# A chain of attention segments: the last outputs' scaling spread over two engines, and two VectorE steps exchanged

## The chip, the cores and the metric

The kernel runs on one core of a Trainium2 chip. A core has several engines, each with its own queue of instructions, worked off in the order in which the program issues them. TensorE (PE, with its weight loads as PEld) multiplies matrices and writes into PSUM, a memory of banks. VectorE (DVE), ScalarE (ACT) and GpSimd (POOL) work on elements; SyncE (SP) only issues transfers. An instruction that needs another engine's result waits on a semaphore, and everything behind it in its queue waits with it. The metric is the time of one execution on the device in microseconds (us), as the median of several.

## The reference

The program is four layers over a sequence of 2048 rows of 640 values: A, B, A, B, each with a layer norm before and a residual sum after. Layer A is attention with a recurrent memory; layer B is a linear attention. The change is in layer A, of which this is the core:

```python
for s in range(n_seg):                       # 64 segments of 32 rows
    h = jnp.concatenate([mem, xs], axis=1)   # 8 memory rows + 32 rows
    q, k, v = (einsum('btd,dhe->bhte', h, W) for W in (Wq, Wk, Wv))   # 32 heads of 192
    p = softmax(where(mask, einsum('bhqe,bhke->bhqk', q, k) * scale, -1e9))
    o = einsum('bhqk,bhke->bhqe', p, v)
    o = einsum('bhte,hed->btd', o, Wo)
    mem = o[:, :M, :]                        # the first 8 rows are the next segment's memory
    outs.append(o[:, M:, :])
```

The memory rows of one segment are an input of the next, so the 64 segments of a layer follow each other strictly, and there are two such layers: 128 segments in all.

## The kernel before, in words

The function `A_chain` (from L1052) runs the segments of a layer. Its instructions stand in each engine's queue in exactly the order of the program text (a manual schedule); waits are made by the framework from what each instruction reads and writes.

A segment handles its 32 heads in four rounds of eight (`NR = 4`, `L = NR - 1` is the last). All rounds share a few buffers. `hT` holds the segment's memory rows and part of its own rows, transposed. In a round, `project` (L1154) multiplies `hT` with the weights for queries, keys and values into the banks `ps_qk_q`, `ps_qk_k` and `ps_v`. `to_rows` (L1172) copies queries and keys out on ScalarE into `raws`, and `turn_rows` (L1177) transposes them in 32x32 blocks on VectorE into `QK` (whose halves are `KT` and `QT`). `scores` (L1194) multiplies them, `weigh` (L1276) takes the exponential into `E` on ScalarE.

The values of a round are cast out of their bank by `v_rows`: half of the bank's partitions (64 rows) by ScalarE (L1184), the other half by VectorE (L1186), both into the tile `Vp`. `attend` (L1207) multiplies `E` with `Vp`; a further column of ones gives the sum of the weights. In the first three rounds the two halves G = 0 and 1 of the outputs lie in one bank `ps_o`; in the last round each has a bank of its own (`ps_o`, and `ps_o1` in the place of the value bank). `weigh_rows` takes the reciprocals of the sums (L1227, in the last round L1231, first G = 1, then G = 0). `scaled` multiplies the outputs with them on their way into `raws`; it has a branch for ScalarE (L1237) and one for VectorE (L1239), which no call used so far. `turn` then transposes the outputs on VectorE (L1372 for the first and third round in one instruction, L1380 for the second and last in two, 192 columns each), and `wo_round` (L1266) multiplies them with the output weights, summed over all rounds into the bank `ps_w`. For the last round's outputs this is 24 products (`ps_w<-arena,QK`): first the 12 that read half G = 1, then the 12 of G = 0. Each half has three chunks of 64 columns; the first four products read the first chunk of G = 1.

The end of a segment is, in the order of the text: the third round's outputs are scaled on ScalarE, turned (L1423, in VectorE's queue as L1372) and the last values are cast (L1424); the last scores and exponentials; 24 products with the second round's outputs and others; `hx_transpose` (L1104), which turns the next segment's own rows into the next `hT`; the last `attend`; the reciprocals; the two scalings (L1440); `keep_values` (L1307), a ScalarE copy that SP then stores; the last turn; 24 products with the third round's outputs (`ps_w<-arena,raws`); the 24 products with the last; in 110 of 128 segments a product for later rows (`next_values`, `ps_x`). Then VectorE turns the memory rows out of `ps_w` (L1453) and adds their two halves into the next `hT` (L1455), and the next segment's queries begin.

The weights that don't stay on the chip are streamed by SP's queue all through the chain, each load released at a set step of TensorE; GpSimd's queue issues the small transfers (`kqb`, `Vp` tails, `xr`, `otb`).

Of the kernel before, what the change touches and what calls it, by code (L numbers as in the profile page):

```python
# [122 lines left out]
class Kernel:  # L123
# [928 lines left out]
    def A_chain(self, xn_dram, at_dram, li, load_slot, piece, late_wo, load_both, wo, low):  # L1052
        nc, tc, KC, NSEG = self.nc, self.tc, self.KC, self.NSEG
        scale = float(self.Dh) ** -0.5
        NR = 4
        with tc.tile_pool(name=f"A{li}_ch", reuse_waits="tile", bufs=1) as sp, \
# [40 lines left out]
            def rounds(s):  # L1097
                return range(NR) if s % 2 == 0 else range(NR - 1, -1, -1)
# [33 lines left out]
            def extra_v(s, n):  # L1132
                r = rounds(s)[n]
                nc.gpsimd.dma_start(out=Vs[n % 2][64:80, :],  # L1134
                                    in_=self.vb_d[s // 8, r].rearrange("g (t s) x f -> s (g t) (x f)", s=8)[s % 8])
# [43 lines left out]
            def v_rows(pv, n, engines):  # L1179
                for x in range(2):  # L1180
                    o = self.two_heads(Vs[n % 2][0:64, 2 * VH * x:2 * VH * x + 2 * VH])
                    i = self.spaced(pv[64 * x:64 * x + 64, 0:384])
                    if engines[x] == "s":
                        nc.scalar.activation(out=o, in_=i, func=ACT.Copy)  # L1184
                    else:
                        nc.vector.tensor_copy(out=o, in_=i)  # L1186
# [47 lines left out]
            def scaled(out, O, rc, G, eng):  # L1234
                i = O[G][:, VH * G:VH * G + 192]
                if eng == "s":
                    nc.scalar.activation(out=out, in_=i, func=ACT.Copy, scale=rc[G])  # L1237
                else:
                    nc.vector.tensor_scalar(out=out, in0=i, scalar1=rc[G], scalar2=None, op0=ALU.mult)  # L1239
# [9 lines left out]
            def tail_rows(rc, rows):  # L1249
                nc.scalar.activation(out=rows, in_=pair[0][:, 0:192], func=ACT.Copy, scale=rc)  # L1250
                return rows
# [80 lines left out]
            for s in range(NSEG):  # L1332
                W = pop.tile([P, 512], F32, name="ps_w", tag="w")
                order = rounds(s)
                L = NR - 1

                def q_or_k(m, n, halves=False):
                    ps = psk if m == "K" else psq
                    project(hT, ps, m, n, s, range(KC))
                    return to_rows(ps, m, halves)  # L1340

                def v_banks():
                    return pop.tile([P, 512], F32, name="ps_v", tag="v")

                def tails_after(n):
                    if n + 2 < NR:
                        extra_v(s, n + 2)
                    elif s + 1 < NSEG:
                        extra_v(s + 1, n + 2 - NR)

                if s > 0:
                    keep_rows(W_done)
                    rows = tail_rows(rct, spare_rows())
                    otb = turn_tail(rows)
                    store_rows(s - 1)
                    store_tail(otb, s - 1, rounds(s - 1)[L])
                turn_rows(q_or_k("Q", 0))
                turn_rows(q_or_k("K", 0))
                pv = v_banks()
                project(hT, pv, "V", 0, s, range(KC))  # L1360
                if s == 0:
                    late_wo(2)
                    late_wo(3, range(OWN // 2))
                v_rows(pv, 0, "sv")
                turn_tails(s)
                OTs = []

                def turn(n, osc):
                    if n in (0, 2):
                        rows = (raw_of["K"][:, 0:384] if n else ots).rearrange("p (c j) -> p c j", j=64)  # L1370
                        OTs.append([rows[:, 3 * G:3 * G + 3, :] for G in range(2)])
                        nc.vector.transpose(out=rows, in_=osc.rearrange("p (c j) -> p c j", j=64))  # L1372
                        return
                    if n == L:
                        OTs.append([KT[:, 3 * G:3 * G + 3, 0:64] for G in range(2)])
                    else:
                        OTs.append([vt[:, VH * G:VH * G + 192].rearrange("p (c j) -> p c j", j=64) for G in range(2)])
                    parts = osc if n == L else [osc[:, 192 * G:192 * G + 192] for G in range(2)]
                    for v, part in list(zip(OTs[n], parts))[::-1 if n == L else 1]:
                        nc.vector.transpose(out=v, in_=part.rearrange("p (c j) -> p c j", j=64))  # L1380

                outs = [(j, i) for j in range(L) for i in range(0, 12 if j else OWN, 2)]

                def output_steps(n):
                    for j, i in outs[0:n]:
                        wo_round(W, order[j], OTs[j], False, False, range(i, i + 2))
                    del outs[0:n]

                for n in range(L):
                    raw = q_or_k("Q", n + 1)  # L1390
                    if n == 2:
                        otb = turn_tail(otr)
                    E = weigh()
                    next_kq(s, n)
                    turn_rows(raw)
                    if n == 1:
                        step = wo_round(W, order[0], OTs[0], True, False, range(OWN, 12))
                        if s == NSEG - 1:
                            load_both(order[L], True)
                            self.kept_tails = []  # L1400
                            self.release(step, 12)
                            tails = self.kept_tails
                        else:
                            load_both(order[L], False)
                    raw = q_or_k("K", n + 1, n + 1 == L)
                    O = attend(E, n)
                    if n != 2:
                        tails_after(n)
                    fetch_kq(s, n)
                    if n == 2:  # L1410
                        store_tail(otb, s, order[1])
                    rc = weigh_rows(O)
                    if n == 1:
                        rct = weigh_tail()
                    turn_rows(raw)
                    if n == L - 1:
                        output_steps(STEPS[0])
                    pv = v_banks()
                    project(hT, pv, "V", n + 1, s, range(KC))
                    osc = raw_of["Q"][:, 0:384]  # L1420
                    for G in range(2):
                        scaled(osc[:, 192 * G:192 * G + 192], O, rc, G, "s")
                    turn(n, osc)  # L1423
                    v_rows(pv, n + 1, "sv")  # L1424
                    if n == 1:
                        otr = tail_rows(rct, raw_of["K"][:, 0:192])
                E = weigh(E)
                tails_after(2)
                next_kq(s, L)
                output_steps(STEPS[1])  # L1430
                if s + 1 < NSEG:
                    hT = new_hT()
                    hx_transpose(hT)
                O = attend(E, L)
                tails_after(L)
                fetch_kq(s, L)
                rc = weigh_rows(O)
                oscs = [raw_of["Q"][:, 192 * G:192 * G + 192] for G in range(2)]
                for G in (1, 0):
                    scaled(oscs[G], O, rc, G, "s")  # L1440
                keep_values()
                turn(L, oscs)
                output_steps(len(outs))
                if s == NSEG - 1:
                    self.spread_tails(0, tails[0], low, "vv")
                if s + 2 < NSEG:
                    load_rows(s + 2)
                wo_round(W, order[L], OTs[L], False, True, (*range(6, 12), *range(6)))
                load_tails(s + 1)
                next_values(s)  # L1450
                if s + 1 < NSEG:
                    wt = raws[:, 0:640].bitcast(F32).rearrange("p (a b t) -> p a b t", a=2, b=KC)
                    nc.vector.transpose(out=wt, in_=W[:, 0:320].rearrange("p (a j b) -> p a b j", a=2, b=KC))  # L1453
                    for a in range(2):
                        nc.vector.tensor_tensor(out=hT[64 * a:64 * a + 64, :, 0:8], in0=wt[0:64, a, :, 0:8],  # L1455
                                                in1=wt[64:P, a, :, 0:8], op=ALU.add)
                rct = weigh_tail()
                W_done = W
# [92 lines left out]
```

## Time and profile before

| what | value |
|---|---|
| median of 3 runs | 3152.37 us (3149.12 to 3162.98) |
| the profiled execution's own time | 3147.72 us |
| its span | 3146.0 us |
| mean granted TensorE clock | 0.993 |
| time from one segment's L1453 to the next, quickest ones | 17.94 us |

The profile is of one execution. A line of the page's groups gives the source line, engine and operation, the tiles written and read, the shapes and the count; behind the first bar the busy time in us and the mean duration of one in ns; behind the second the time that the engine had been idle just before, and who released it. A line of a timeline gives start and duration in us from the start of the span, an `xN` for merged neighbours, and in brackets the idle time before with its releaser. A line of the chain of waits gives start and duration of one piece of the path that ended last. A line of the waits gives who waited for whom, the total in us, how often, and the longest. Durations of products overlap, since TensorE starts the next before the last has come out.

### The profile page before, as it was taken

What the parts mean: (1) busy time and instruction counts of PE and PEld (TensorE: products, weight loads), DVE (VectorE), ACT (ScalarE), POOL (GpSimd) and SP (SyncE); (2) the same over time, 40 slices, a digit from 0 to 9 for tenths busy, and PEclk for the clock granted to TensorE, in tenths of its full rate; (3) what the DMA queues carried; (4) which work ended last, traced back from release to release, by engine and by line L of the source; (5) the groups of instructions that cost most, each with busy time, mean ns of one, the idle gap of its engine ahead of it and who ended that gap; (6) DMA issues with size and microseconds to landing.
All of it is one profiled execution on the core that took longest, in us unless ns stands there. A gap on an engine that the chain in (4) does not pass through costs nothing.

```text
span 3146.0 us, 141467 instructions
## 1 busy us (share of the span) xinstructions
PE 2989.4 (95%) x59552; PEld 1917.3 (61%) x59586; DVE 2180.7 (69%) x5420; ACT 1909.3 (61%) x4540; POOL 1388.6 (44%) x2867
## 2 busy tenths in 40 slices
PE   9899999999999999899999999999999999998999
PEld 7666666666666666555377666666666666665553
DVE  5577777777777777566644677777777777775665
ACT  3366666666666666556433666666666666665553
POOL 3255555555555555430112555555555555554300
PEclk9999999999999999999999999999999999999999
DMA  9877777877777787830378777777777777778300
GB/s 378 314 246 260 264 255 253 267 259 244 263 262 252 244 269 259 290 122 1 119 261 321 251 254 267 259 242 261 263 254 249 260 262 250 260 261 292 110 1 34
DMA packets 331783, 741.78 MB, mean 236 GB/s; under 512 B 67186, under 2 KB 108394, under 8 KB 328076
## 3 DMA queue, kind: packets, MB, share of 16 engines
q1 hardware_dynamic: 262252, 629.72, 57.8%
q0 software_dynamic: 68032, 99.38, 10.9%
q8 instruction: 469, 7.68, 1.0%
q10 hardware_dynamic: 864, 3.64, 0.3%
q14 instruction: 166, 1.36, 0.1%
HBM read 662.90 MB, written 70.14 MB: 233 GB/s over the span
## 4 chain that ended last, share of the span: by engine, by line
PE 76%; DVE 8%; DMA 8%; issue 3%; ACT 3%; POOL 1%; SPq 0%; DVEq 0%; POOLq 0%; ACTq 0%
PE ps_qk_k L1154 13%; PE ps_qk_q L1154 13%; PE ps_v L1154 12%; PE ps_w L1266 10%; PE ps_s L1194 6%; PE ps_pre L981 6%; PE ps_o L1207 2%; PE kv L1506 2%; DMA arena<-in_A_Wo_dram 2%; PE ps_wo L466 2%; DVE raws L1453 2%; ACT raws L1237 2%; DVE hT L1455 2%; PE ps_pq L517 2%; PE ps_t L1220 1%
## 5 line engine op out<-in xcount | busy, mean ns | idle before, releaser
L1154 PEld LDWEIGHTS <-hT 128*32 128x32 bf16 x30720 | 786.3, 96 | 458.3 <-DVE hT L1455 78.9
L1177 DVE STREAM_TRANSPOSE QK<-raws 128x512 bf16<-128x512 bf16 (+1 forms) x1152 | 729.6, 642 | 202.5 <-ACT raws L1172 164.1
L1130 POOL COPY QK<-kqb 64x192 bf16<-64x192 bf16 x1024 | 350.8, 343 | 468.7 <-PE ps_s L1194 261.5
L1154 PE MATMUL ps_qk_q<-arena,hT 128*32 128x384 bf16 x10240 | 509.9, 327 | 36.6 <-DVE hT L1455 28.2
L1154 PE MATMUL ps_qk_k<-arena,hT 128*32 128x384 bf16 x10240 | 509.7, 327 | 3.7 <-issue 2.8
L1172 ACT ACTIVATE raws<-ps_qk_k 128x512 bf16<-128x512 f32 (+1 forms) x640 | 313.6, 511 | 252.0 <-PE ps_qk_k L1154 245.1
L1237 ACT ACTIVATE raws<-ps_o,under 128x192 bf16<-128x192 f32 x1024 | 374.5, 421 | 113.3 <-DVE under L1231 98.5
L1154 PE MATMUL ps_v<-arena,hT 128*32 128x384 bf16 x8192 | 429.5, 326 | 6.2 <-issue 3.8
L1134 POOL DMA_DIRECT2D Vp<-vb x512 | 258.3, 504 | 326.3 <-PE ps_t L1220 214.8
L1172 ACT ACTIVATE raws<-ps_qk_q 128x512 bf16<-128x512 f32 x512 | 305.9, 598 | 156.7 <-PE ps_qk_q L1154 142.9
L1123 POOL DMA_DIRECT2D kqb<-kqb x512 | 292.8, 572 | 84.1 <-POOL QK L1130 59.4
L1186 DVE CAST Vp<-ps_v 64x384 bf16<-64x384 f32 x512 | 286.2, 559 | 25.3 <-ACT Vp L1184 9.2
L1194 PEld LDWEIGHTS <-QK 128*80 128x80 bf16 x4096 | 195.3, 120 | 167.6 <-issue 156.8
L1266 PE MATMUL ps_w<-arena,under 128*32 128x320 bf16 x6144 | 280.4, 300 | 4.9 <-issue 2.6
L1184 ACT ACTIVATE Vp<-ps_v 64x384 bf16<-64x384 f32 x512 | 247.0, 483 | 35.9 <-PE ps_v L1154 34.6
L1194 PE MATMUL ps_s<-QK 128*80 128x80 bf16 x4096 | 252.3, 209 | 5.3 <-DVE QK L1177 4.6
L1276 ACT ACTIVATE E<-ps_s 80x320 bf16<-80x320 f32 x512 | 217.9, 426 | 28.9 <-PE ps_t L1220 28.8
L1119 POOL DMA_DIRECT2D attn<-under x128 | 91.7, 716 | 265.9 <-DVE under L1115 231.2
L981 PEld LDWEIGHTS <-arena 128*128 128x128 bf16 x1920 | 187.9, 98 | 31.3 <-issue 4.1
L1112 ACT ACTIVATE raws<-ps_w 64x160 f32<-64x160 f32 x256 | 76.8, 300 | 205.9 <-DVE raws L1453 204.4
L1207 PE MATMUL ps_o<-Vp,E 80*32 80x193 bf16 x4096 | 179.6, 247 | 8.1 <-issue 3.9
L1266 PE MATMUL ps_w<-arena,QK 128*32 128x320 bf16 x3072 | 135.0, 304 | 36.2 <-DVE QK L1380 23.6
(166 smaller groups left out, 4362.1 us busy)
## 6 DMA issues: line engine op xcount, KB each, us to landing
arena<-in_A_Wo_dram SPq DMA_DIRECT2D x560, 320.0 KB
arena<-in_A_Wq_dram SPq DMA_DIRECT2D x427, 384.0 KB
arena<-in_A_Wk_dram SPq DMA_DIRECT2D x298, 384.0 KB
arena<-in_A_Wv_dram SPq DMA_DIRECT2D x290, 384.0 KB
kqb<-kqb POOLq DMA_DIRECT2D x512, 48.0 KB, 4.3
kqb<-arena POOLq DMA_DIRECT2D x14, 1536.0 KB, 9.5
Vp<-vb POOLq DMA_DIRECT2D x512, 24.2 KB, 3.6
otb<-otb POOLq DMA_DIRECT2D x256, 48.0 KB, 4.0
```

What stands on the lines that cost most here:

```text
L981: nc.tensor.matmul(ps[:, T * i:T * i + T], lhsT=w[b][:, P * c:P * c + P], rhs=xBT[:, b, :], start=(b == 0), stop=(b == KC - 1))
L1123: nc.gpsimd.dma_start(out=kqb[:], in_=self.kqb_d[r, :, s, :])
L1130: nc.gpsimd.tensor_copy(out=o, in_=kqb[h, :].rearrange("p (x c q) -> p x c q", c=3, q=16))
L1134: nc.gpsimd.dma_start(out=Vs[n % 2][64:80, :], in_=self.vb_d[s // 8, r].rearrange("g (t s) x f -> s (g t) (x f)", s=8)[s % 8])
L1154: last = nc.tensor.matmul(o, lhsT=hT[:, b, :], rhs=rhs, start=(i == 0), stop=(i == KC - 1), tile_position=(0, 32 * g), skip_group_check=True)
L1172: nc.scalar.activation(out=raw[:, c], in_=ps[:, c], func=ACT.Copy)
L1177: nc.vector.transpose(out=o, in_=i)
L1184: nc.scalar.activation(out=o, in_=i, func=ACT.Copy)
L1186: nc.vector.tensor_copy(out=o, in_=i)
L1194: nc.tensor.matmul(S[0:80, c0:c0 + 80], lhsT=KT[:, 4 * x + c, :], rhs=QT[:, 4 * x + c, :], start=(c % 2 == 0), stop=(c % 2 == 1), skip_gro ...
L1237: nc.scalar.activation(out=out, in_=i, func=ACT.Copy, scale=rc[G])
L1266: step = nc.tensor.matmul(W[q:q + 32, 0:320], lhsT=OT[i // 6][:, i % 6 // 2, 32 * (i % 2):32 * (i % 2) + 32], rhs=rhs, start=(first and i ...
```

## The change

Three edits, all in the end of a segment:

- In the round before the last, the cast of the last round's values (`v_rows`) is issued ahead of the turn of the third round's outputs instead of behind it. In VectorE's queue the two change places; on ScalarE nothing changes place, as the turn has no part there.
- Of the last outputs, half G = 1 is scaled by VectorE (a `tensor_scalar` out of PSUM with the reciprocal as a column), half G = 0 still by ScalarE.
- The turn of half G = 1 is made in two instructions, first the chunk of 64 columns that the first products read, then the other 128 columns; half G = 0 in one as before.

```diff
-                    for v, part in list(zip(OTs[n], parts))[::-1 if n == L else 1]:
-                        nc.vector.transpose(out=v, in_=part.rearrange("p (c j) -> p c j", j=64))
+                    pieces = ((1, 0, 1), (1, 1, 3), (0, 0, 3)) if n == L else ((0, 0, 3), (1, 0, 3))
+                    for G, a, b in pieces:
+                        nc.vector.transpose(out=OTs[n][G][:, a:b, :], in_=parts[G].rearrange("p (c j) -> p c j", j=64)[:, a:b, :])
...
                         scaled(osc[:, 192 * G:192 * G + 192], O, rc, G, "s")
+                    if n + 1 == L:
+                        v_rows(pv, n + 1, "sv")
                     turn(n, osc)
-                    v_rows(pv, n + 1, "sv")
+                    if n + 1 < L:
+                        v_rows(pv, n + 1, "sv")
...
                 for G in (1, 0):
-                    scaled(oscs[G], O, rc, G, "s")
+                    scaled(oscs[G], O, rc, G, "v" if G else "s")
```

## The prediction

> **What bounds the kernel now.** I read the page first, then the chain of waits of one segment, then the timelines of VectorE, ScalarE and TensorE over the end of that segment.
>
> ```profile
> span 3146.0 us, 141467 instructions
> PE 2989.4 (95%) x59552; PEld 1917.3 (61%) x59586; DVE 2180.7 (69%) x5420; ACT 1909.3 (61%) x4540; POOL 1388.6 (44%) x2867
> PE 76%; DVE 8%; DMA 8%; issue 3%; ACT 3%; POOL 1%; SPq 0%; DVEq 0%; POOLq 0%; ACTq 0%
> ...
> L1266 PE MATMUL ps_w<-arena,QK 128*32 128x320 bf16 x3072 | 135.0, 304 | 36.2 <-DVE QK L1380 23.6 <-DMA arena<-in_A_Wo_dram 8.8 <-issue 3.3
> ```
>
> TensorE is busy for 95% of the span and carries 76% of the chain. An edit on VectorE and ScalarE therefore matters only where TensorE stands still for them. The last row is such a place: the products with the last outputs of a segment (`ps_w<-arena,QK`, 24 in each of 128 segments). The chain through the end of one segment, start and duration in us:
>
> ```profile
> 615.58 0.18 PE ps_o L1207 x4
> 615.76 0.02 issue
> 615.78 0.26 DVE under L1231 x2
> 616.05 0.43 ACT raws L1237
> 616.48 0.02 issue
> 616.50 0.39 DVE QK L1380
> 616.89 0.04 issue
> 616.93 1.03 PE ps_w L1266 x24
> 617.96 0.02 issue
> 617.99 0.53 DVE raws L1453
> ```
>
> From the last attention product the path leaves TensorE for two reciprocals, one scaling on ScalarE and one turn (a 32x32 block transpose) on VectorE, comes back for the 24 products, and then goes to the turn that makes the next segment's memory rows. The same stretch on VectorE, on ScalarE and on TensorE:
>
> ```profile
> 613.35 0.77 DVE L1177 STREAM_TRANSPOSE QK<-raws 128x256 bf16<-128x256 bf16 x2
> 614.25 0.58 DVE L1372 STREAM_TRANSPOSE raws<-raws 128x384 bf16<-128x384 bf16 x1
> 614.86 0.56 DVE L1186 CAST Vp<-ps_v 64x384 bf16<-64x384 f32 x1
> 615.34 0.35 DVE L1104 STREAM_TRANSPOSE hT<-xr 128x160 bf16<-128x160 bf16 x1
> 615.78 0.25 DVE L1231 RECIPROCAL under<-ps_o 128x1 f32<-128x1 f32 x2
> 616.50 0.69 DVE L1380 STREAM_TRANSPOSE QK<-raws 128x192 bf16<-128x192 bf16 x2 [0.47 <-ACT raws L1237]
> 617.99 0.52 DVE L1453 STREAM_TRANSPOSE raws<-ps_w 128x320 f32<-128x320 f32 x1 [0.79 <-PE ps_w L1266]
> 618.54 0.43 DVE L1455 TENSOR_TENSOR hT<-raws 64x40 bf16<-64x40 f32 x2
> ```
> ```profile
> 613.48 0.74 ACT L1237 ACTIVATE raws<-ps_o,under 128x192 bf16<-128x192 f32 x2
> 614.19 0.48 ACT L1184 ACTIVATE Vp<-ps_v 64x384 bf16<-64x384 f32 x1
> ...
> 616.05 0.73 ACT L1237 ACTIVATE raws<-ps_o,under 128x192 bf16<-128x192 f32 x2 [0.74 <-DVE under L1231]
> 616.67 0.49 ACT L1307 ACTIVATE under<-ps_x 128x384 bf16<-128x384 f32 x1
> ```
> ```profile
> 615.47 0.35 PE L1207 MATMUL ps_o<-Vp,E 80*32 80x193 bf16 x8
> ...
> 615.72 1.00 PE L1266 MATMUL ps_w<-arena,raws 128*32 128x320 bf16 x24
> 616.93 1.00 PE L1266 MATMUL ps_w<-arena,QK 128*32 128x320 bf16 x24 [0.21 <-DVE QK L1380]
> ```
>
> Three things are to be seen. VectorE runs from 613.35 almost without a break to 615.69 (615.34 + 0.35) and is free only 0.09 before the reciprocals. From there on everything hangs on it and on ScalarE. And TensorE could start its last 24 products earlier than they come: 24 products take 1.00 with about 0.30 for the last alone, so six groups of four start 0.14 apart, and after 615.72 the next slot would be at 615.72 + 6 x 0.14 = 616.56. They start at 616.93, so 0.37 a segment is the most that a faster end can win.
>
> **The change part by part.** *Last values' cast ahead of the third outputs' turn.* On VectorE L1186 goes ahead of L1372. Nothing is added, no DMA moves, ScalarE's order stays. What counts is what the cast waits for. Its other half, L1184, reads the same bank `ps_v` on ScalarE. In the typical segment ScalarE's half ends at 614.67 and VectorE's starts at 614.86, with the turn in between as cover. A segment whose values came late shows it uncovered, and behind it stands the group of all these casts with its idle time and releaser:
>
> ```profile
> 1293.94 0.58 DVE L1372 STREAM_TRANSPOSE raws<-raws 128x384 bf16<-128x384 bf16 x1
> 1295.37 0.56 DVE L1186 CAST Vp<-ps_v 64x384 bf16<-64x384 f32 x1 [0.85 <-ACT Vp L1184]
> ```
> ```profile
> 1294.85 0.48 ACT L1184 ACTIVATE Vp<-ps_v 64x384 bf16<-64x384 f32 x1 [0.94 <-PE ps_v L1154]
> ```
> ```profile
> L1186 DVE CAST Vp<-ps_v 64x384 bf16<-64x384 f32 x512 | 286.2, 559 | 25.3 <-ACT Vp L1184 9.2
> ```
>
> The bank was full before 1294.85, since ScalarE read it then; VectorE was idle and still waited until ScalarE's half was done (1295.33) and 0.04 more. So the two halves go one after the other in this program, and the turn that now fills the wait is moved behind it. In the typical segment: VectorE is free at 614.12 and waits; the cast starts at 614.67 + 0.03 = 614.70, only 0.16 sooner. The next turn starts 0.48 behind a cast (614.86 to 615.34), at 615.18, and ends at 615.76; its reader, the products of 615.72, starts at 615.81, which costs nothing as TensorE has 0.37 to spare. Two turns of 0.378 together take 0.69, so one overlaps the next by 0.07: the turn of the next rows (L1104) starts at 615.18 + 0.58 - 0.07 = 615.69 and ends at 616.04. The reciprocals, behind it in VectorE's queue, start at 616.07 instead of 615.78: **0.29 later**. What they waited for before (TensorE's attention, 615.76) is no longer last. The attention itself, which waits for the cast's end (615.42 + 0.05 = 615.47), may start 0.05 sooner, which is then hidden.
>
> *Scaling side by side and the turn in two pieces.* Prices from these rows:
>
> ```profile
> L1380 DVE STREAM_TRANSPOSE QK<-raws 128x192 bf16<-128x192 bf16 x256 | 88.4, 378 | 59.3 <-ACT raws L1237 59.3
> L1372 DVE STREAM_TRANSPOSE raws<-raws 128x384 bf16<-128x384 bf16 x128 | 74.0, 578 | 17.1 <-ACT raws L1237 2.3
> L492 DVE TENSOR_TENSOR arena<-ps_v,rk 128x500 bf16<-128x500 f32 x64 | 40.8, 655 | 3.5 <-PE ps_v L466 3.3
> L492 DVE TENSOR_TENSOR arena<-ps_v,rk 128x140 bf16<-128x140 f32 x64 | 16.0, 292 | 0.0
> ```
>
> No VectorE scaling out of PSUM at 192 columns is in the trace. The nearest rows are products out of PSUM: 292 at 140 columns and 655 at 500, so 292 + 52 x 1.01 = 0.345; I take 0.35, with 0.29 and the 0.56 of the cast as outer bounds. Turns cost 1.04 ns a column (578 - 378 over 192), so 64 columns take 0.245 and 128 take 0.31; a piece could cost as little as 0.18 (0.245 less the overlap) and no more than the 0.378 of the undivided one. [...]
>
> New end, with 0.03 from one VectorE step to one that needs it (618.51 to 618.54): scaling 616.07 + 0.17 + 0.03 = 616.27 to 616.62; first piece 616.65 to 616.90; second 616.83 to 617.14; the other half's turn 617.07 to 617.45 (ScalarE's scaling, about 616.43 to 616.85, is done). TensorE, 0.05 behind each: first group 616.95, second and third 617.19 and 617.33, fourth 617.50, sixth 617.78. Before, the sixth started at 616.93 + 5 x 0.14 = 617.63. **0.15 later**. The second part alone would have won about 0.13 (the same sum from 615.78 gives 617.49); the first gives back 0.29. ScalarE's L1307, on whose end a store in SP's queue waits, moves from 616.67 to about 616.75, and SP's loads behind it by as much; POOL's load into `xr` comes over 1 us behind L1104 and is covered.
>
> ```profile
> PE ps_w L1266 <- DVE QK L1380: 23.6, 106, 0.8
> PE ps_w L1266 <- DMA arena<-in_A_Wo_dram: 12.8, 17, 2.8
> SPq L261 <- ACT under L1307: 460.6, 110, 5.5
> ```
>
> In 106 segments TensorE waited for the last turn; in others weights came last, and there a later turn costs nothing. 106 x 0.15 = 16 us. The profiled execution took 3147.7 us (span 3146.0); the sum is 3164. The median of the runs shown, 3152.4, lies 4.7 above it, so I give 3169.
>
> **The rivals.** *1. The cast does not really wait for ScalarE's half.* Then it runs beside it at 614.20, the turn ends at 615.26, L1104 at 615.54, the attention starts 0.05 earlier and so do the reciprocals, and the second part keeps its gain: 0.13 + 0.05 = 0.18 by 106, so 19 us less: 3133. Against it: the row with 0.85 of idle. For it: in the typical segment the cast's start is explained by the turn alone. It decides when the cast can start before about 614.40. [...]
>
> *2. The delay is absorbed.* A weight load late in one segment gets 0.15 more, so TensorE's other waits for DMA shrink; or the new VectorE steps are at their low ends (0.29 and 0.18), which takes 0.06 + 0.06 off. Then 0.03 a segment or nothing: 3152 to 3157, no measurable change. For it: DMA waits stand in the rows above; against it: they touch few segments.
>
> *3. The scalings are not side by side.* Both write `raws`, as the two casts both write `Vp`. If ScalarE's half waits for VectorE's, it runs from 616.68 to 617.10, the last turn starts at 617.13, and 0.06 more is lost: 106 x 0.21 = 22 us, 3175. With the scaling at 0.56 as well, 0.42 a segment: 3197.
>
> **How the numbers follow.** A change under 0.5% (16 us) can't be told from none here, and my likeliest value stands on that border. Chances: longer hand-over as summed, 0.08 to 0.25 a segment (3161 to 3179) 0.60, a little over half of it beyond the border; rival 3 or dearer VectorE steps (3175 to 3197) 0.16; absorbed 0.14; rival 1 0.10. So slower 0.33 + 0.16 and a little for a slow second part, 0.50; no change 0.27 + 0.14 - 0.01, 0.40; faster 0.10. The range goes from 3146, which leaves rival 1 out, to 3192, which leaves out the dearest steps. The likeliest case's own range is 3161 to 3179.
>
> **What would show it.** Right: the idle time before L1186 grows from 25 us to about 95 (0.70 - 0.12 = 0.58 in most of 128 segments), released by ScalarE's L1184; reciprocals L1231 start right behind L1104, with no idle time released by TensorE; a VectorE scaling of about 0.35; first piece about 0.245; TensorE's waits for the last turn grow. Wrong: the cast starting beside L1184, or reciprocals as early as before, or the last 24 products spread over less than 0.85.

## The result and the profile after

The changed kernel takes 3160.5 us (median of 22 runs) against 3155.4 us for the kernel before on the same chips; the ratio is 1.0024, 95% interval 1.0013 to 1.0036, so 4 to 11 us more, about 7.5 by the ratio (the two medians alone lie 5.1 apart). The change makes the kernel a little slower, by less than half a percent. The profiled execution has a span of 3152.3 us at a granted clock of 0.992.

The chain of waits through the end of one segment of the changed kernel (start, duration, engine and line):

```profile
617.00 0.47 ACT Vp L1184
617.46 0.02 issue
617.49 0.56 DVE Vp L1186
618.05 0.48 DVE raws L1372
618.53 0.24 DVE hT L1104
618.77 0.03 issue
618.80 0.23 DVE under L1231 x2
619.03 0.40 DVE raws L1239
619.43 0.02 issue
619.46 0.26 DVE QK L1381
619.71 0.04 issue
619.75 1.08 PE ps_w L1266 x24
```

Before, the last attention product on TensorE (`ps_o`) led straight to the reciprocals. Now the chain comes to them through ScalarE's half of the cast, VectorE's half, the third outputs' turn and the turn of the next rows, one behind the other in VectorE's queue. The timeline of VectorE over the same stretch shows what it waits for:

```profile
616.13 0.77 DVE L1177 STREAM_TRANSPOSE QK<-raws 128x256 bf16<-128x256 bf16 x2
617.49 0.56 DVE L1186 CAST Vp<-ps_v 64x384 bf16<-64x384 f32 x1 [0.58 <-ACT Vp L1184]
617.97 0.56 DVE L1372 STREAM_TRANSPOSE raws<-raws 128x384 bf16<-128x384 bf16 x1
618.46 0.31 DVE L1104 STREAM_TRANSPOSE hT<-xr 128x160 bf16<-128x160 bf16 x1
618.80 0.23 DVE L1231 RECIPROCAL under<-ps_o 128x1 f32<-128x1 f32 x2
619.00 0.42 DVE L1239 TENSOR_SCALAR raws<-ps_o,under 128x192 bf16<-128x192 f32 x1
619.46 0.70 DVE L1381 STREAM_TRANSPOSE QK<-raws 128x64 bf16<-128x64 bf16 x3
620.86 0.52 DVE L1457 STREAM_TRANSPOSE raws<-ps_w 128x320 f32<-128x320 f32 x1 [0.71 <-PE ps_w L1266]
```

VectorE now stands idle for 0.58 until ScalarE's half is done, and the work that used to fill this time follows later. The hand-over to the next segment (L1457, L1453 before) comes at 620.86; the one before it in this trace came at 602.83, 18.04 earlier. In the kernel before an undisturbed segment took 17.94 (600.05 to 617.99). The groups of the lines concerned:

```profile
L1186 DVE CAST Vp<-ps_v 64x384 bf16<-64x384 f32 x512 | 286.2, 559 | 100.6 <-ACT Vp L1184 88.8
L1266 PE MATMUL ps_w<-arena,QK 128*32 128x320 bf16 x3072 | 141.2, 305 | 29.7 <-DVE QK L1381 16.0 <-DMA arena<-in_A_Wo_dram 9.5 <-issue 3.1
L1239 DVE TENSOR_SCALAR raws<-ps_o,under 128x192 bf16<-128x192 f32 x128 | 53.5, 418 | 0.0
L1381 DVE STREAM_TRANSPOSE QK<-raws 128x192 bf16<-128x192 bf16 x128 | 42.9, 335 | 0.0
L1104 DVE STREAM_TRANSPOSE hT<-xr 128x160 bf16<-128x160 bf16 x126 | 39.0, 310 | 0.0
L1381 DVE STREAM_TRANSPOSE QK<-raws 128x128 bf16<-128x128 bf16 x128 | 34.4, 269 | 0.0
L1381 DVE STREAM_TRANSPOSE QK<-raws 128x64 bf16<-128x64 bf16 x128 | 31.4, 246 | 4.4
L1231 DVE RECIPROCAL under<-ps_o 128x1 f32<-128x1 f32 x256 | 30.3, 160 | 8.6 <-PE ps_o L1207 4.9
```

The idle time ahead of the casts went from 25.3 to 100.6 us, 88.8 of it released by ScalarE's half. That ahead of the reciprocals fell from 24.8 to 8.6, and the part of it that TensorE's attention released from 16.3 to 4.9: TensorE was waited for 42 times before and 11 times now, and in most segments they stand right behind L1104. The wait in the kernel before:

```profile
DVE under L1231 <- PE ps_o L1207: 16.3, 42, 1.6
```

In what follows, a *quick segment* is the shortest time that recurs from one hand-over to the next: the median of those within 0.05 us of the quickest, of the 124 intervals within the two layers. I take it as the time of a segment in which nothing is late. It repeats to 0.01 us (four of the kernels were run again with other loads, see below, and gave the same values), while the whole time of the kernel scatters by some 20 us between runs. Quick segments and their number come from one profiled execution of each kernel; the ratio is to the kernel before on the same chip, and where its interval holds 1 the whole time can't be told from that of the kernel before.

| kernel | quick segment | how many of 124 | ratio to before, 95% interval |
|---|---|---|---|
| before | 17.94 | 40 | 1 |
| changed | 18.04 | 46 | 1.0024 (1.0013 to 1.0036) |
| only the cast ahead of the turn | 18.175 | 37 | 1.0072 (1.0051 to 1.0092) |
| only the new end | 17.80 | 26 | 0.9975 (0.9962 to 0.9987) |
| only the scaling on two engines | 17.88 | 26 | 0.9998 (0.9984 to 1.0012) |
| only the turn in two pieces | 17.86 | 25 | 0.9975 (0.9959 to 0.9990) |
| changed, values in a second bank | 17.74 | 28 | 0.9959 (0.9943 to 0.9976) |
| second bank, old order, new end | 17.78 | 23 | 0.9974 (0.9956 to 0.9991) |
| changed, rows' turn late | 17.80 | 18 | 0.9991 (0.9977 to 1.0005) |

### The profile page after: what moved, and what is told of

The parts are those of the page before. It is cut to its first block, busy times and chain, and to the rows that moved or that the text cites. A ratio compares the mean times of both kernels' runs of the same rounds, so it can differ in the third digit from the quotient of the medians.

```text
span 3152.3 us, 141500 instructions
## 1 busy us (share of the span) xinstructions
PE 3009.4 (95%) x59586; PEld 1895.3 (60%) x59586; DVE 2210.4 (70%) x5676; ACT 1869.1 (59%) x4412; POOL 1391.7 (44%) x2867
## 4 chain that ended last, share of the span: by engine, by line
PE 71%; DVE 13%; DMA 7%; ACT 5%; issue 3%; POOL 1%; SPq 0%; DVEq 0%; POOLq 0%; ACTq 0%
PE ps_qk_k L1154 13%; PE ps_qk_q L1154 13%; PE ps_v L1154 10%; PE ps_w L1266 8%; PE ps_pre L981 5%; PE ps_s L1194 5%; DMA arena<-in_A_Wo_dram 2%; PE kv L1510 2%; DVE raws L1457 2%; PE ps_wo L466 2%; PE ps_o L1207 2%; ACT raws L1237 2%; DVE hT L1459 2%; DVE Vp L1186 2%; PE ps_pq L517 2%
## 5 line engine op out<-in xcount | busy, mean ns | idle before, releaser
L1237 ACT ACTIVATE raws<-ps_o,under 128x192 bf16<-128x192 f32 x896 | 334.5, 422 | 149.8 <-DVE under L1231 133.5
L1186 DVE CAST Vp<-ps_v 64x384 bf16<-64x384 f32 x512 | 286.2, 559 | 100.6 <-ACT Vp L1184 88.8
L1184 ACT ACTIVATE Vp<-ps_v 64x384 bf16<-64x384 f32 x512 | 247.0, 482 | 34.4 <-PE ps_v L1154 33.3
## 6 DMA issues: line engine op xcount, KB each, us to landing
Vp<-vb POOLq DMA_DIRECT2D x512, 24.2 KB, 3.7
```

## The experiments

My theory was that the change is two effects of opposite sign: the exchange of cast and turn makes what stands behind them in VectorE's queue late, since the cast waits for ScalarE's half; the new end wins back about half. The first rival was that the exchange is harmless and the new end costs the time.

**The two parts alone.** The exchange alone:

```diff
+                    if n + 1 == L:
+                        v_rows(pv, n + 1, "sv")
                     turn(n, osc)
-                    v_rows(pv, n + 1, "sv")
+                    if n + 1 < L:
+                        v_rows(pv, n + 1, "sv")
```

> The kernel before with the last values' cast ahead of the third outputs' turn and nothing else. In the traces, quick segments take 17.94 us in the kernel before and 18.04 in the changed one. Theory (the cast waits for ScalarE's half, so what is queued behind it on VectorE comes late): the last reciprocals start 0.24 later as in the changed kernel, and with the old end all of it reaches the hand-over: quick segments 18.15 to 18.20, the time 15 to 30 us above before. Rival (the exchange is harmless, the new end with its VectorE scaling and three turns costs the time): quick segments 17.94, no change within 5 us.

Measured: quick segments 18.175 and 1.0072, 23 us. The timeline of VectorE in this kernel has the old end behind the late reciprocals:

```profile
606.82 0.56 DVE L1186 CAST Vp<-ps_v 64x384 bf16<-64x384 f32 x1 [0.58 <-ACT Vp L1184]
607.30 0.56 DVE L1372 STREAM_TRANSPOSE raws<-raws 128x384 bf16<-128x384 bf16 x1
607.79 0.31 DVE L1104 STREAM_TRANSPOSE hT<-xr 128x160 bf16<-128x160 bf16 x1
608.13 0.23 DVE L1231 RECIPROCAL under<-ps_o 128x1 f32<-128x1 f32 x2
608.85 0.69 DVE L1380 STREAM_TRANSPOSE QK<-raws 128x192 bf16<-128x192 bf16 x2 [0.48 <-ACT raws L1237]
610.34 0.52 DVE L1456 STREAM_TRANSPOSE raws<-ps_w 128x320 f32<-128x320 f32 x1 [0.80 <-PE ps_w L1266]
```

The reciprocals come 15.98 behind the last hand-over (592.15 to 608.13) instead of 15.73 (600.05 to 615.78), and all of these 0.24 to 0.25 reach the next hand-over (610.34 - 592.15 = 18.19, against 17.94; 0.235 over the quick segments). The rival falls. The other part alone:

```diff
-                    for v, part in list(zip(OTs[n], parts))[::-1 if n == L else 1]:
-                        nc.vector.transpose(out=v, in_=part.rearrange("p (c j) -> p c j", j=64))
+                    pieces = ((1, 0, 1), (1, 1, 3), (0, 0, 3)) if n == L else ((0, 0, 3), (1, 0, 3))
+                    for G, a, b in pieces:
+                        nc.vector.transpose(out=OTs[n][G][:, a:b, :], in_=parts[G].rearrange("p (c j) -> p c j", j=64)[:, a:b, :])
...
-                    scaled(oscs[G], O, rc, G, "s")
+                    scaled(oscs[G], O, rc, G, "v" if G else "s")
```

> The kernel before with the scaling on two engines and the first half's turn in two pieces, and the old order of cast and turn. Theory: this part alone wins about 0.13 a segment, quick segments 17.78 to 17.84, the time 8 to 18 us below before. Rival (the new end costs the time): quick segments at 18.04, the time 5 to 10 us above before.

Measured: quick segments 17.80, which is 0.136 less, and 0.9975, 8 us less. So +0.235 and -0.136 make the +0.10 of the whole change: the parts add up.

**What of the new end does it.** First the second half of that diff without the pieces, then the pieces without the VectorE scaling.

```diff
-                    scaled(oscs[G], O, rc, G, "s")
+                    scaled(oscs[G], O, rc, G, "v" if G else "s")
```

> The kernel before with half G = 1 scaled on VectorE, half G = 0 on ScalarE, and each half still turned in one instruction. Quick segments: 17.94 before, 17.80 with the whole new end. Theory (the time from the reciprocals to the first turn's end bounds the hand-over; VectorE's scaling starts 0.06 sooner and takes as long as ScalarE's): a third to a half of the gain, quick segments 17.86 to 17.90, the time 2 to 8 us below before. Rival (scaling side by side brings nothing, the pieces are all): quick segments 17.94.

```diff
-                    for v, part in list(zip(OTs[n], parts))[::-1 if n == L else 1]:
+                    pieces = ((1, 0, 1), (1, 1, 3), (0, 0, 3)) if n == L else ((0, 0, 3), (1, 0, 3))
+                    for G, a, b in pieces:
```

> The kernel before with the first half's turn in two pieces and both scalings on ScalarE. Theory: the first products start 0.13 sooner, the second piece then bounds; quick segments 17.84 to 17.89, the time 2 to 9 us below before. Rival (the third turn instruction eats the gain): quick segments 17.94 or longer.

Measured: 17.88 and 17.86, as expected; each wins 0.06 to 0.08 and together they win 0.136. The time of the first did not follow (0.9998, where 2 to 8 us less was expected); the second's did (0.9975). The half loads below bear on why the whole time answers so unevenly, but they were not run for these two kernels, so for the first it stays open.

**Why the cast waits.** Both halves read one bank and write one tile. In this kernel the values' products for partitions 64 to 127 go into the queries' bank, which is empty by then; the output tile stays shared.

```diff
+                        elif n == NR - 1 and g > 1:
+                            o = psq[32 * g:32 * g + 32, :].rearrange("p (x c) -> p x c", x=2)[:, :, 64:256]
...
+                    if n == NR - 1 and x:
+                        i = psq[64:P, :].rearrange("p (e c) -> p e c", e=2)[:, :, 64:256].rearrange("p e (f j) -> p e j f", j=6)
```

> The changed kernel, but in the last round the values' products for partitions 64 to 127 go into the bank of the queries, which is empty by then, so that the two halves of the cast read different banks. Both halves still write the same tile. Theory (the wait comes from the shared bank): VectorE's half starts beside ScalarE's, the cast no longer holds up the queue, the reciprocals wait for TensorE again; quick segments 17.70 to 17.80, the time 10 to 24 us below before. Rival (the wait comes from the shared output tile, or from elsewhere): VectorE's half still starts 0.03 behind ScalarE's end, quick segments 18.04, 5 to 12 us above before.

Measured: quick segments 17.74 and 0.9959, 13 us less than before. VectorE and ScalarE of this kernel (its lines lie up to 4 further down in the file):

```profile
814.39 0.77 DVE L1179 STREAM_TRANSPOSE QK<-raws 128x256 bf16<-128x256 bf16 x2
815.26 0.56 DVE L1190 CAST Vp<-ps_qk_q 64x384 bf16<-64x384 f32 x1
815.74 0.56 DVE L1376 STREAM_TRANSPOSE raws<-raws 128x384 bf16<-128x384 bf16 x1
816.23 0.33 DVE L1104 STREAM_TRANSPOSE hT<-xr 128x160 bf16<-128x160 bf16 x1
816.76 0.25 DVE L1235 RECIPROCAL under<-ps_o 128x1 f32<-128x1 f32 x2 [0.20 <-PE ps_o L1211]
```
```profile
815.21 0.48 ACT L1188 ACTIVATE Vp<-ps_v 64x384 bf16<-64x384 f32 x1
```

The casts now run side by side (815.21 and 815.26) into the same tile, the idle time of 0.58 is gone, and the reciprocals wait for TensorE again. So the wait came from the shared bank and not from the shared output tile. (The second bank is also another tile; this run doesn't part bank and tile on the side of the input.) The traces say more: in the changed kernel the cast's instruction itself waits on the semaphore that ScalarE raises, and ScalarE's half ended the idle time ahead of the casts 134 times (88.8 us); in the second-bank kernel it did so twice (0.9 us), and ahead of the last casts TensorE's products did so 32 times (16.0 us). The wait thus stands in the program; no run here shows that the chip needs it. This version is quicker than both kernels. The same with the turn ahead of the cast as in the kernel before (that order, the second bank and the new end):

> The new end and the second bank for the last values' upper half, but the old order: the third outputs' turn ahead of the cast. Theory (bank and order only help together: with the turn ahead the cast starts where it did, at the turn's end): quick segments 17.80 as with the new end alone, against 17.74 with bank and order together; time 5 to 14 us below before. Rival (the second bank alone gives the gain): quick segments 17.74.

Measured: 17.78 and 0.9974, nearer to the theory than to the rival. Without the exchange the second bank wins 0.02 (17.80 to 17.78); with the exchange in place it wins 0.30 (18.04 to 17.74). Bank and exchange together win 0.07 over the new end alone. So in the quick segments the exchange pays only with the second bank, and then 0.05 (17.78 to 17.74); in the whole time the two second-bank kernels can't be told apart, as their intervals overlap.

**Is it the queue?** The changed kernel with the turn of the next rows moved behind the last outputs' turns:

```diff
-                if s + 1 < NSEG:
-                    hT = new_hT()
-                    hx_transpose(hT)
                 O = attend(E, L)
...
                 turn(L, oscs)
+                if s + 1 < NSEG:
+                    hT = new_hT()
+                    hx_transpose(hT)
```

> The changed kernel with the turn of the next segment's own rows (L1104) moved behind the last outputs' turns on VectorE. Theory (a queue on VectorE: cast, outputs' turn and rows' turn stand ahead of the reciprocals): with one of the three away the reciprocals start about 0.24 to 0.30 earlier, quick segments 17.78 to 17.86, 7 to 18 us below before. Rival (the cast or the attention products behind it are what is late, not the queue): quick segments stay at 18.04.

```profile
860.15 0.56 DVE L1186 CAST Vp<-ps_v 64x384 bf16<-64x384 f32 x1 [0.58 <-ACT Vp L1184]
860.63 0.56 DVE L1372 STREAM_TRANSPOSE raws<-raws 128x384 bf16<-128x384 bf16 x1
861.22 0.23 DVE L1231 RECIPROCAL under<-ps_o 128x1 f32<-128x1 f32 x2
```

The cast waits as before, but with one step fewer ahead of them the reciprocals come 15.74 behind the hand-over at 845.48, and quick segments take 17.80. The queue is what matters, as expected. The time did not follow: 3 us less by the ratio, with an interval that holds no change, where 7 to 18 were expected, and just 18 segments were quick (in a profiled execution that, with 3166 us, was the longest of twelve). What held the others was not settled for this kernel.

**Where part of the difference went.** 126 hand-overs (63 in each layer) by 0.10 would be 12.6 us; 7.5 were measured. By 0.136, 17 us; 8 were measured. Of these three kernels, the shorter the quick segments, the fewer they are (46, 40, 26 of 124), though the kernel with the longest, only the cast ahead, has just 37. So I suspected the streamed weights: whoever is early waits for them, whoever is late finds them there. Four kernels load only half of each streamed piece during the chain:

```diff
-                self.last_load = nc.sync.dma_start(out=slot[m, b], in_=wview[m][:, b, PW * r:PW * r + PW])
+                rows = 64 if self.half else P
+                self.last_load = nc.sync.dma_start(out=slot[m, b][0:rows], in_=wview[m][0:rows, b, PW * r:PW * r + PW])
...
-            self.last_load = nc.sync.dma_start(out=into[:, c:c + 1280], in_=wov[r, G, :, o:o + 1280])
+            rows = P if into is wo_kept else 64
+            self.last_load = nc.sync.dma_start(out=into[0:rows, c:c + 1280], in_=wov[r, G, 0:rows, o:o + 1280])
```

> The kernel before, but the weights streamed during the chain are loaded for 64 of 128 partitions only (the other half keeps what lay there, so a part of the products is made with other weights). Theory (weights that arrive late swallow a part of each gain and of each loss): the streamed bytes halved, most segments take the quick 17.94 us instead of 40 of 124, and the time falls by 20 to 55 us. Rival (the slow segments have another cause): less than 10 us gained, as few quick segments as before.

Measured: 3121.9 us where the kernel before took 3150.4 on that chip, and 100 of 124 segments quick. The page's rates over the span, before and with half loads, show what the halved streams took away: 242 to 269 GB/s in the two chains became 139 to 153 (of the 40 slices, 3 to 16 and 23 to 36 lie in the chains):

```profile
GB/s 378 314 246 260 264 255 253 267 259 244 263 262 252 244 269 259 290 122 1 119 261 321 251 254 267 259 242 261 263 254 249 260 262 250 260 261 292 110 1 34
```
```profile
GB/s 374 297 144 147 153 147 145 151 150 141 153 149 144 149 152 139 240 95 1 123 263 296 144 144 151 149 146 149 152 147 144 153 148 143 153 146 218 99 1 34
```

So most of the slow segments (84 of 124, against 24 with half loads) were slow because of the streams. Whether the weights themselves came late or the streams held up other transfers, these runs don't part. The changed kernel and its two parts with the same loads:

> The changed kernel with the same halved loads. Quick segments are 0.10 longer than in the kernel before. Theory (late weights hide the difference): with most segments quick, it lies 10 to 13 us (126 x 0.10) above the kernel before with halved loads. Rival (the difference is the 5 to 8 us that was measured with full loads, whatever the weights do): 5 to 8 us.

Measured: 3134.7, 12.8 us above the half-load kernel before; quick segments 18.04.

> The kernel before with only the new end, and the halved loads. Quick segments are 0.136 shorter than in the kernel before. Theory: 14 to 17 us (126 x 0.136 at most) below the kernel before with halved loads. Rival: 7 to 10 us, as measured with full loads.

Measured: 3106.0, 15.8 us below; quick segments 17.80.

> The kernel before with only the cast moved ahead, and the halved loads. Quick segments are 0.235 longer than in the kernel before. Theory: 26 to 30 us (126 x 0.235 at most) above the kernel before with halved loads. Rival: 21 to 24 us, as measured with full loads.

Measured: 3140.7, 18.8 us above; quick segments 18.18. The first two show the full difference, as the theory has it (with four executions each: 3120 to 3124 us before, 3131 to 3137 changed, 3100 to 3112 with the new end). The third fits neither theory nor rival: of 126 x 0.235 = 29.6 us only 18.8 came, no more than with full loads (23, interval 16 to 29). Of the missing part about 5 us is seen in TensorE's waits for the turned queries and keys, half-load kernel before first (lines of these kernels lie 4 further down):

```profile
PE ps_s L1198 <- DVE QK L1181: 10.8, 12, 1.3
```
```profile
PE ps_s L1198 <- DVE QK L1181: 5.8, 9, 1.2
```

These few long waits are shorter in the slowest of the four kernels alone; in the changed kernel with half loads they are 10.8 again. The rest, some 6 us, stays open.

The traces can be asked the same from the other side, for one execution of each kernel. What the 124 intervals take beyond the quick one sums to 53.0 us in the kernel before and 46.1 in the changed one, so about 7 of 124 x 0.10 = 12.4 us come back in the slow segments; with the new end alone it is 74.3, which in that execution (4 us above the median) eats the whole gain of 124 x 0.136 = 16.9. With half loads the three sums are 24.2, 24.4 and 27.4, and little or nothing comes back. With only the cast ahead it is 58.2 with full loads and 15.5 with half, the other way round. So absorption by the streams is seen for the changed kernel and for the new end; for the cast alone the runs don't settle it.

## Why the prediction was right, and where it was off

The forecast was 3169 us, 16 us more than before, from +0.15 a segment over 106 segments. It came to +7.5 us with +0.10 in an undisturbed segment. Direction and mechanism were right and the size was about twice too large: +0.10 lies inside the 0.08 to 0.25 a segment of the likeliest case, but 7.5 us lie just below the 8.5 (106 x 0.08) that this would give, and 3160.5 just below that case's own 3161 to 3179. So the result fell on the near side of the border of 0.5% on which the forecast stood, and not on the far side, to which I had given the larger chance.

- *The cast waits for ScalarE's half.* Right: idle time ahead of L1186 of 100.6 us (about 95 was forecast), released by L1184. The reason is the shared bank, as the second bank shows, by a wait in the program. No run here tried the two halves of the cast on one bank without the program's wait.
- *The reciprocals come 0.29 later.* This step was mis-sized: 0.24. I had taken L1104 at the 0.35 that it took before and its start at 0.51 behind the turn; right behind a turn it took 0.31 and started 0.49 behind it.
- *The new end wins 0.13 to 0.14.* Right in size, 0.136 alone, but partly by luck, as its terms were off in both directions and the errors cancel: the VectorE scaling took 0.418, more than the 0.35 that I took for it (and no quicker than ScalarE's 0.421), while the second piece and the last turn took 0.269 and 0.335 instead of 0.31 and 0.378. The first piece took 0.246 as forecast.
- *106 hand-overs count in full.* This step was off in the same direction, though by little: 106 x 0.10 = 10.6 us lies inside the 4 to 11 that were measured. With the streams halved the changed kernel does pay 12.8 us, near 126 x 0.10; with full streams only 7.5. I had taken off the 20 or so segments in which weights came last for the last products, which is 2 us of the 5 between the two; the other 3 are no more than the noise of the whole time. That was my rival of absorption, and it took a part, not all.
- *TensorE's waits for the last turn grow.* Wrong: 23.6 us before, 16.0 after. The products with the third outputs start later, as their turn was moved (618.59 - 602.83 = 15.76 behind the hand-over, against 615.72 - 600.05 = 15.67). As forecast this costs nothing, since they still end (618.59 + 1.00 = 619.59) before the last turn's first piece does (619.71), but it fills a part of that wait. The loss is what the last 24 products show: they start 0.04 later (619.75 - 602.83 = 16.92 behind the hand-over, against 616.93 - 600.05 = 16.88) and are spread over 0.06 more, since the second piece, which ends at 619.89, is not ready when the first four are done, and the next four start 0.19 behind them where the later ones follow 0.14 apart:

```profile
618.59 1.00 PE L1266 MATMUL ps_w<-arena,raws 128*32 128x320 bf16 x24
619.75 1.06 PE L1266 MATMUL ps_w<-arena,QK 128*32 128x320 bf16 x24 [0.17 <-DVE QK L1381]
```

- *The rival that the scalings are not side by side* fell: ScalarE's started at 619.13, inside VectorE's 619.00 to 619.42, although both write `raws`. *The rival that the cast doesn't wait* fell as a forecast, but it is the second-bank kernel: 3133 was the sum for it. That kernel's quick segments are 0.20 shorter than before, against the 0.18 of the sum, and its time 13 us shorter, against 19.

## What to carry to other kernels

Before a step is moved ahead in a queue, look for what it waits for where that is hidden now: a step that seems to start right behind its neighbour may be covered by it, and one segment in which the cover was missing (a cast with 0.85 of idle time) gave the wait away before the move was made. In this program two engines that empty one bank take turns (VectorE's cast starts 0.03 behind the end of ScalarE's); giving each its own bank turned a loss of 0.10 a segment into a gain of 0.20. And where weights are streamed just in time, a gain or a loss on the path may appear in the total only in part (here 7.5 of 12.6 us and 8 of 17), so compare the undisturbed segments first and the totals afterwards.

## What was not expected of the hardware

Here a VectorE turn that another engine's result released was longer than the same turn right behind its neighbour. The turn of 192 columns took 0.378 where ScalarE's scaling released it, and 0.335 where it did not, as the last of the three here; in the kernel with only the scaling on two engines the two turns together took 0.64, against 0.69 before. The rows' turn, which waits in none of these kernels, took 0.354 behind the cast (before), 0.310 behind the third outputs' turn (changed) and 0.329 behind that same turn with the second bank, on average. Why is not shown. Scaling 128x192 values out of PSUM with a column of factors took VectorE 418 ns and ScalarE 421 ns, so VectorE was no faster at it. What its scaling won by itself (0.06) is an earlier start: 15.94 behind the hand-over, right behind the reciprocals, where ScalarE's first one began at 16.00.
